# Transposing two bf16 tokens as one 32-bit word, with all inputs loaded as 4 KB pieces, in a gated recurrence kernel

## The chip, the cores and the metric

The kernel runs on one core of one Trainium2 chip. The metric is the device time of one execution in microseconds (us). Engines are called as the profile calls them: PE (matrix multiply; PEld is its weight load), DVE (vector), ACT (activation functions), POOL (GpSimd), SP (it issues the DMAs). Fast executions of one kernel on one chip differ by up to about 1.5% here (316.87 to 321.59 us for the kernel before). Runs further above the fastest of their kernel (up to 327.44) count as slow and are left out of every comparison. A ratio comes with a 95% interval; the record's verdict at a margin of 2% (faster, same, slower, unclear) is given with it.

## The reference

A gated linear recurrence over time, followed by a causal convolution gate and two small matrix products, for 4 sequences of 6336 tokens with 256 channels:

```
a   = exp(8 * sigmoid(r) * log(sigmoid(a_param)))
h_t = a_t * h_(t-1) + sqrt(1 - a_t^2) * sigmoid(i_t) * x_t        (y = h)
out = (sigmoid(conv5(y)) * (y @ w_val)) @ w_out
```

x, r and i (26 MB each) are read and out (26 MB) is written, all in fp32 with a token's 256 channels as one row of 1 KB.

## The kernel before

The inputs arrive with tokens on the 128 partitions. The kernel runs the recurrence with channels on the partitions and time along the row. So PE transposes the tanh of r (for a), the factor n = sqrt(1 - a^2) (back to tokens), and the finished product u (to channels). All engines follow one static order, computed ahead from a table of costs; each engine works its own list strictly in order. Sigmoids are computed as tanh.

```python
nc.sync.dma_start(ri[:, 0, ...], rf[t0:t0 + nt, :].rearrange("(w p j) d -> p w j d", ...))   # r: 4 KB pieces
nc.sync.dma_start(ri[:, 1, ...], if_[t0:t0 + nt, :].rearrange("(k p) d -> p k d", p=P))      # i: 1 KB pieces
nc.sync.dma_start(xt[...],       xf[t0:t0 + nt, :].rearrange("(k p) d -> p k d", p=P))       # x: 1 KB pieces
...
# tanh of r and i in one instruction, 2 x 1024 fp32 elements per partition, to bf16
nc.scalar.activation(out=tring[...], in_=ri[:, :, w, 0:nj, :], func=ACT.Tanh, scale=0.5)
# u2: u = (tanh(i) + 1) * x, per tile on DVE (one instruction) or on POOL (two)
nc.vector.scalar_tensor_tensor(out=u, in0=ti, scalar=1.0, in1=xt, op0=ALU.add, op1=ALU.mult)
nc.gpsimd.tensor_scalar(out=t1, in0=ti, scalar1=1.0, scalar2=1.0, op0=ALU.mult, op1=ALU.add)
nc.gpsimd.tensor_tensor(out=u, in0=t1, in1=xt, op=ALU.mult)
...
for j in range(nj):                                # one bf16 transpose per 128 tokens and half of the channels
    nc.tensor.transpose(out=dst[:, col:col + P], in_=src[:, j, h * P:(h + 1) * P], identity=ident_b[:])
```

i and x come in 1 KB pieces because the scan needs time in order. With token `k*128 + p` on partition `p`, a transposed block is 128 consecutive tokens. With four consecutive tokens per partition, each block would hold every fourth token.

## Time and profile before

| | before |
|---|---|
| time, median (range of 2 runs) | 320.12 us (319.77 to 320.48) |
| span of the profiled run | 317.1 us |
| busy: ACT, DVE, PE, POOL | 290.1, 270.4, 246.2, 224.6 us |
| DMA packets on the main queue | 65904 |

The page and the windows are shown in the prediction. The chain of work that ended last, by engine:

```profile
ACT 25%; DMA 23%; DVE 21%; PE 13%; issue 10%; POOL 4%; SPq 1%; DVEq 0%; ACTq 0%; POOLq 0%
```

Two groups of instructions (line, engine, operation, operands, count | busy us, mean ns | idle before them and what ended it): tanh, and DVE's product with x.

```profile
L351 ACT ACTIVATE tring<-ri 128x2048 bf16<-128x2048 f32 x48 | 90.7, 1919 | 7.7 <-DMA ri<-in_i_gate_dram 7.7
...
L360 DVE SCALAR_TENSOR_TENSOR uring<-tring,xt 128x1024 bf16<-128x1024 bf16 x15 | 24.4, 1624 | 8.2 <-DMA xt<-in_x_dram 8.2
```

And two bursts of PE's transposes from the timeline (start us, length us):

```profile
182.22 1.07 PE L397 MATMUL bank<-ident_b,ering 128*128 128x128 bf16 x16 [0.54 <-ACT ering L388]
...
191.90 1.06 PE L332 MATMUL bank<-ident_b,tring 128*128 128x128 bf16 x16
```

The reader should see that DMA is 23% of the chain of work that ended last. DVE's product lasts 1624 ns on average though its shortest instance takes 1198 ns. Sixteen bf16 transposes take 1.06 us, of which about 0.22 us is the length of the last: (1.06 - 0.22)/15 = 0.056 us each.

### The profile page before, as it was taken

What the parts mean: (1) busy time and instruction counts of PE and PEld (TensorE: products, weight loads), DVE (VectorE), ACT (ScalarE), POOL (GpSimd) and SP (SyncE); (2) the same over time, 40 slices, a digit from 0 to 9 for tenths busy, and PEclk for the clock granted to TensorE, in tenths of its full rate; (3) what the DMA queues carried; (4) which work ended last, traced back from release to release, by engine and by line L of the source; (5) the groups of instructions that cost most, each with busy time, mean ns of one, the idle gap of its engine ahead of it and who ended that gap; (6) DMA issues with size and microseconds to landing.
All of it is one profiled execution on the core that took longest, in us unless ns stands there. A gap on an engine that the chain in (4) does not pass through costs nothing.

```text
span 317.1 us, 7227 instructions
## 1 busy us (share of the span) xinstructions
PE 246.2 (78%) x2987; PEld 163.6 (52%) x2987; DVE 270.4 (85%) x269; ACT 290.1 (91%) x231; POOL 224.6 (71%) x140
## 2 busy tenths in 40 slices
PE   1262877687679768897989798959977997999994
PEld 1141745453546446564655375627644665655662
DVE  3125799999597998999999999997998999999892
ACT  6789999899969999999998999899989999998963
POOL 6329551869469536999989999999997289868000
PEclk9999999999759999999999999997999999999997
DMA  8999999999999999999999999996999994853334
GB/s 208 340 365 380 367 368 382 386 345 352 394 322 349 389 356 375 350 391 385 357 382 382 393 369 383 393 389 191 395 385 383 385 379 164 262 189 133 135 154 179
DMA packets 67327, 104.55 MB, mean 330 GB/s; under 512 B 3287, under 2 KB 54238, under 8 KB 67294
## 3 DMA queue, kind: packets, MB, share of 16 engines
q1 hardware_dynamic: 65904, 103.82, 91.8%
q0 software_dynamic: 1376, 0.26, 1.0%
q8 instruction: 23, 0.38, 0.5%
q14 instruction: 10, 0.08, 0.1%
q10 hardware_dynamic: 14, 0.01, 0.0%
HBM read 78.39 MB, written 25.95 MB: 329 GB/s over the span
## 4 chain that ended last, share of the span: by engine, by line
ACT 25%; DMA 23%; DVE 21%; PE 13%; issue 10%; POOL 4%; SPq 1%; DVEq 0%; ACTq 0%; POOLq 0%
DMA ri<-in_i_gate_dram 15%; DVE yring L425 9%; ACT tring L351 8%; DMA xt<-in_x_dram 6%; DVE gv L477 5%; ACT ering L388 5%; PE bank L489 4%; ACT tg L459 4%; ACT aring L376 4%; PE gp L451 3%; DVE osb L500 3%; PE bank L397 3%; POOL uring L364 2%; DMA ri<-in_r_gate_dram 2%; DVE uring L404 2%
## 5 line engine op out<-in xcount | busy, mean ns | idle before, releaser
L384 POOL TENSOR_TENSOR ering<-aring 128x1024 f32<-128x1024 f32 (+2 forms) x56 | 97.1, 1753 | 55.0 <-ACT aring L376 52.8
L425 DVE TENSOR_TENSOR_SCAN yring<-aring,yring,bank 128x1024 bf16<-128x1024 f32 (+5 forms) x54 | 110.1, 2052 | 0.7 <-PE bank L332 0.5
L351 ACT ACTIVATE tring<-ri 128x2048 bf16<-128x2048 f32 (+1 forms) x51 | 93.9, 1868 | 7.8 <-DMA ri<-in_i_gate_dram 7.7
L364 POOL TENSOR_TENSOR uring<-t,xt 128x1024 bf16<-128x1024 f32 (+1 forms) x36 | 83.6, 2323 | 9.9 <-DMA xt<-in_x_dram 7.3
L451 PE MATMUL gp<-yring,diag 64*64 64x512 bf16 (+14 forms) x1196 | 67.9, 350 | 6.7 <-ACT tg L459 4.6
L489 PE MATMUL bank<-wo,gv 128*128 128x256 bf16 x396 | 57.3, 279 | 18.5 <-DVE gv L477 8.2
L477 DVE SCALAR_TENSOR_TENSOR gv<-tg,val 128x1024 bf16<-128x1024 bf16 (+1 forms) x54 | 60.3, 1120 | 6.7 <-ACT tg L459 4.5
L376 ACT ACTIVATE aring<-bank,khf 128x1024 f32<-128x1024 bf16 (+2 forms) x56 | 59.6, 1111 | 3.3 <-PE bank L332 2.5
L459 ACT ACTIVATE tg<-gp 128x1024 bf16<-128x1024 f32 (+1 forms) x51 | 51.1, 1003 | 7.1 <-PE gp L451 6.8
L489 PEld LDWEIGHTS <-gv 128*128 128x128 bf16 x396 | 36.0, 99 | 37.9 <-issue 16.4
L467 PE MATMUL val<-yring,wv 128*128 128x512 bf16 (+1 forms) x204 | 51.5, 376 | 0.8 <-DVE gv L477 0.8
L500 DVE COPY osb<-bank 128x512 f32<-128x512 f32 x69 | 45.6, 679 | 3.8 <-PE bank L489 3.3
L451 PEld LDWEIGHTS <-diag 64*64 64x64 bf16 x1196 | 30.9, 108 | 33.0 <-issue 16.5
L388 ACT ACTIVATE ering<-ering,b 128x2048 bf16<-128x2048 f32 (+4 forms) x15 | 46.7, 3112 | 0.3
L332 PE MATMUL bank<-ident_b,tring 128*128 128x128 bf16 x396 | 31.3, 231 | 18.5 <-ACT tring L351 13.0
L397 PE MATMUL bank<-ident_b,ering 128*128 128x128 bf16 x396 | 32.9, 240 | 15.8 <-ACT ering L388 12.5
L404 DVE TENSOR_TENSOR uring<-bank,uring 128x1024 bf16<-128x1024 bf16 (+1 forms) x51 | 33.4, 669 | 11.8 <-PE bank L397 11.6
L363 POOL TENSOR_SCALAR t<-tring 128x1024 f32<-128x1024 bf16 (+1 forms) x36 | 40.1, 1115 | 2.6 <-ACT tring L351 1.2
L397 PEld LDWEIGHTS <-ering 128*128 128x128 bf16 x396 | 28.1, 108 | 23.3 <-ACT ering L388 15.5
L332 PEld LDWEIGHTS <-tring 128*128 128x128 bf16 x396 | 25.7, 103 | 27.7 <-ACT tring L351 15.1
L332 PE MATMUL bank<-ident_b,uring 128*128 128x128 bf16 x396 | 30.4, 226 | 3.3 <-DVE yring L425 1.8
L360 DVE SCALAR_TENSOR_TENSOR uring<-tring,xt 128x1024 bf16<-128x1024 bf16 x15 | 24.4, 1624 | 8.2 <-DMA xt<-in_x_dram 8.2
(32 smaller groups left out, 112.6 us busy)
## 6 DMA issues: line engine op xcount, KB each, us to landing
out_dram<-osb SPq DMA_DIRECT2D x48, 512.0 KB, 7.1
ri<-in_r_gate_dram SPq DMA_DIRECT2D x23, 1024.0 KB, 8.1
ri<-in_i_gate_dram SPq DMA_DIRECT2D x23, 1024.0 KB, 11.8
xt<-in_x_dram SPq DMA_DIRECT2D x23, 1024.0 KB, 10.7
ri<-in_r_gate_dram SPq DMA_DIRECT2D x2, 512.0 KB, 5.9
ri<-in_i_gate_dram SPq DMA_DIRECT2D x2, 512.0 KB, 8.1
xt<-in_x_dram SPq DMA_DIRECT2D x2, 512.0 KB, 8.1
ri<-in_r_gate_dram SPq DMA_DIRECT2D x3, 256.0 KB, 2.9
```

Source lines behind the costliest of these rows:

```text
L332: nc.tensor.transpose(out=dst[:, col:col + P], in_=src[:, j, h * P:(h + 1) * P], identity=ident_b[:])
L351: nc.scalar.activation(out=tring[:, r:i + 1:i - r, 0:nj, :], in_=ri[:, :, w, 0:nj, :], func=ACT.Tanh, scale=0.5)
L364: nc.gpsimd.tensor_tensor(out=u, in0=t1, in1=xt, op=ALU.mult)
L376: nc.scalar.activation(out=aring[:, h, a0:a0 + nt].rearrange("c (w p j) -> c w p j", p=P, j=nj), in_=live.pop(("srT", k))[:, 0:nt].rearran ...
L384: nc.gpsimd.tensor_tensor(out=ering[:, h, e0:e0 + nt], in0=a, in1=a, op=ALU.mult)
L388: nc.scalar.activation(out=nring[:, :, 2 * e0:2 * e0 + m], in_=ering[:, :, e0:e0 + m], func=ACT.Sqrt, scale=-0.25, bias=b025[:, 0:1])
L397: nc.tensor.transpose(out=nT[:, j, h * P:(h + 1) * P], in_=nring[:, h, n0 + j * P:n0 + (j + 1) * P], identity=ident_b[:])
L425: nc.vector.tensor_tensor_scan(out=yring[:, h, y0 + c0:y0 + c1], data0=aring[:, h, a0 + c0:a0 + c1], data1=xT[:, c0:c1], initial=0.0 if fr ...
L451: nc.tensor.matmul(out=gp[64 * h:64 * h + 64, m, c0:c1], lhsT=diag[rows, h, kk, rows], rhs=yring[rows, h, src:src + c1 - c0], start=(sh == 0),
L459: nc.scalar.activation(out=tg[:, :, 0:nt], in_=live.pop(("gp", g))[:, :, 0:nt], func=ACT.Tanh, scale=0.5)
L477: nc.vector.scalar_tensor_tensor(out=gv[:, 0:nj, hs, :].rearrange("c j h p -> c j (h p)"), in0=tg[:, hs, 0:nt].rearrange("c h (p j) -> c j ...
L489: nc.tensor.matmul(out=ops[:, e * D:(e + 1) * D], lhsT=gv[:, 2 * i + e, hk, :], rhs=wo[:, hk, :], start=(hk == 0), stop=(hk == H - 1))
```

## The change

A pair of bf16 values of two consecutive tokens is one 32-bit word. PE transposes it as an fp32 element and both tokens stay next to each other. With four tokens per partition that is two word transposes, placed at every second word of the output, and time is in order. So all three inputs can be loaded as 4 KB pieces, and 1188 transposes become 594. The price: tanh and u2 must interleave two tokens, which lie 1 KB apart in the input. a_param is transposed in two 16-bit halves.

```diff
-        nc.sync.dma_start(ri[:, 1, ...], if_[...].rearrange("(k p) d -> p k d", p=P))
+        nc.sync.dma_start(ri[:, 0:nw, 1, 0:nj, :], by_token(if_, c))    # "(w p j) d -> p w j d", r and x alike
 ...
-                for j in range(nj):
-                    nc.tensor.transpose(out=dst[:, col:col + P], in_=src[:, j, h * P:(h + 1) * P], identity=ident_b[:])
+                for w in range(nj // 2):          # src and dst seen as 32-bit words
+                    nc.tensor.transpose(out=dst[:, at + w:at + nw * P:nw],
+                                        in_=src[:, w * D + h * P:w * D + (h + 1) * P], identity=ident_f[:])
 ...                                               # tanh: e, the token of the pair, is innermost
+                out=tring[...].rearrange("p s (w d e) -> p s w d e", d=D, e=2),
+                in_=ri[:, w, :, 0:nj, :].rearrange("p s (w e) d -> p s w d e", e=2), func=ACT.Tanh, scale=0.5)
 ...                                               # u2: xt, ti and u in the same order; on DVE
-                nc.vector.scalar_tensor_tensor(out=u, in0=ti, scalar=1.0, in1=xt, ...)
+                for k in range(nj // 2):
+                    nc.vector.scalar_tensor_tensor(out=u[:, k], in0=ti[:, k], scalar=1.0, in1=xt[:, k], ...)
```

(Not shown: the setup of a_param, nT with words read at every second place, exp reading contiguously. The order of operations and the table of costs are unchanged.)

More of the change, by code (lines that the diff above doesn't have):

```diff
@@ L242, with by_token @@
     live = {}
+    def by_token(src, c):
+        t0, nt, g0, g1 = chunks[c]
+        return src[t0:t0 + nt, :].rearrange("(w p j) d -> p w j d", w=g1 - g0, p=P)
     def load(c):
@@ L247, in load @@
         ri = inp.tile([P, 2, 2, SUB, D], FP32, name="ri", tag="ri", bufs=NIN)
-        nc.sync.dma_start(ri[:, 0, 0:nw, 0:nj, :], rf[t0:t0 + nt, :].rearrange("(w p j) d -> p w j d", w=nw, j=nj))
-        nc.sync.dma_start(ri[:, 1, 0:nw, 0:nj, :].rearrange("p w j d -> p (w j) d"),
-                          if_[t0:t0 + nt, :].rearrange("(k p) d -> p k d", p=P))
+        nc.sync.dma_start(ri[:, 0:nw, 0, 0:nj, :], by_token(rf, c))
+        nc.sync.dma_start(ri[:, 0:nw, 1, 0:nj, :], by_token(if_, c))
         live["ri", c] = ri
@@ L255, in loadx @@
         t0, nt, g0, g1 = chunks[c]
-        xt = inp.tile([P, 2 * SUB, D], FP32, name="xt", tag="xt", bufs=NX)
-        nc.sync.dma_start(xt[:, 0:nt // P, :], xf[t0:t0 + nt, :].rearrange("(k p) d -> p k d", p=P))
+        nw, nj = g1 - g0, nt // (g1 - g0) // P
+        xt = inp.tile([P, 2, SUB, D], FP32, name="xt", tag="xt", bufs=NX)
+        nc.sync.dma_start(xt[:, 0:nw, 0:nj, :], by_token(xf, c))
         live["xt", c] = xt
@@ L271 @@
         make_identity(nc, ident_f[:])
-        ident_b = const.tile([P, P], BF16, name="ident_b")
-        nc.vector.tensor_copy(out=ident_b[:], in_=ident_f[:])
         b025 = const.tile([P, 1], FP32, name="b025")
@@ L288 @@
         with tc.tile_pool(name="ps_setup", bufs=1, space=bass.MemoryType.PSUM) as ps_setup:
-            kps = ps_setup.tile([P, H], FP32, name="kps")
-            nc.tensor.transpose(out=kps[:], in_=ap2[0:H, :], identity=ident_f[0:H, 0:H])
+            U32 = mybir.dt.uint32
+            ap2h = const.tile([H, 2, P], FP32, name="ap2h")
+            nc.vector.tensor_scalar(out=ap2h[:, 0, :].bitcast(U32), in0=ap2[:].bitcast(U32), scalar1=16, scalar2=None,
+                                    op0=ALU.logical_shift_right)
+            nc.vector.tensor_scalar(out=ap2h[:, 1, :].bitcast(U32), in0=ap2[:].bitcast(U32), scalar1=0xFFFF, scalar2=None,
+                                    op0=ALU.bitwise_and)
+            kph = ps_setup.tile([P, 2, H], FP32, name="kph")
+            for k in range(2):
+                nc.tensor.transpose(out=kph[:, k, :], in_=ap2h[0:H, k, :], identity=ident_f[0:H, 0:H])
+            kps = const.tile([P, H], FP32, name="kps")
+            nc.vector.tensor_scalar(out=kps[:].bitcast(U32), in0=kph[:, 0, :].bitcast(U32), scalar1=16, scalar2=None,
+                                    op0=ALU.logical_shift_left)
+            nc.vector.tensor_tensor(out=kps[:].bitcast(U32), in0=kps[:].bitcast(U32), in1=kph[:, 1, :].bitcast(U32),
+                                    op=ALU.bitwise_or)
             kexp = const.tile([P, H], FP32, name="kexp")
@@ L317, with bank @@
         psum = ctx.enter_context(tc.tile_pool(name="psum", bufs=1, space=bass.MemoryType.PSUM))
-        def bank(b, dtype):
-            return psum.tile([P, WIN * 4 // mybir.dt.size(dtype)], dtype, name=f"bank{b}", tag=f"bank{b}", bufs=1)
+        def bank(b):
+            return psum.tile([P, WIN], FP32, name=f"bank{b}", tag=f"bank{b}", bufs=1)
         aring = rings.tile([P, H, NS * WIN], FP32, name="aring")
@@ L323 @@
         nring = ering[:].bitcast(BF16)
-        tring = rings.tile([P, NTR + NTI, SUB, D], BF16, name="tring")
-        uring = rings.tile([P, NU, SUB, D], BF16, name="uring")
+        tring = rings.tile([P, NTR + NTI, SUB * D], BF16, name="tring")
+        tring_w = tring[:].bitcast(FP32)
+        uring = rings.tile([P, NU, SUB * D], BF16, name="uring")
+        uring_w = uring[:].bitcast(FP32)
         yring = rings.tile([P, H, NY * WIN], BF16, name="yring")
         def transposes(dst, srcs, h):
-            col = 0
+            at = 0
             for src, nj in srcs:
-                for j in range(nj):
-                    nc.tensor.transpose(out=dst[:, col:col + P], in_=src[:, j, h * P:(h + 1) * P],
-                                        identity=ident_b[:])
-                    col += P
+                nw = nj // 2
+                for w in range(nw):
+                    nc.tensor.transpose(out=dst[:, at + w:at + nw * P:nw], in_=src[:, w * D + h * P:w * D + (h + 1) * P],
+                                        identity=ident_f[:])
+                at += nw * P
         def op_load(g, eng):
@@ L350, in op_tanh @@
             r, i = g % NTR, NTR + g % NTI
-            nc.scalar.activation(out=tring[:, r:i + 1:i - r, 0:nj, :], in_=ri[:, :, w, 0:nj, :], func=ACT.Tanh, scale=0.5)
+            nc.scalar.activation(
+                out=tring[:, r:i + 1:i - r, 0:nj * D].rearrange("p s (w d e) -> p s w d e", d=D, e=2),
+                in_=ri[:, w, :, 0:nj, :].rearrange("p s (w e) d -> p s w d e", e=2), func=ACT.Tanh, scale=0.5)
         def op_u2(g, eng):
@@ L356, in op_u2 @@
             w = g - chunks[c][2]
-            xt, ti = live["xt", c][:, w * nj:(w + 1) * nj, :], tring[:, NTR + g % NTI, 0:nj, :]
-            u = uring[:, g % NU, 0:nj, :]
+            xt = live["xt", c][:, w, 0:nj, :].rearrange("p (w e) d -> p w d e", e=2)
+            ti = tring[:, NTR + g % NTI, 0:nj * D].rearrange("p (w d e) -> p w d e", d=D, e=2)
+            u = uring[:, g % NU, 0:nj * D].rearrange("p (w d e) -> p w d e", d=D, e=2)
             if eng == "DVE":
-                nc.vector.scalar_tensor_tensor(out=u, in0=ti, scalar=1.0, in1=xt, op0=ALU.add, op1=ALU.mult)
+                for k in range(nj // 2):
+                    nc.vector.scalar_tensor_tensor(out=u[:, k], in0=ti[:, k], scalar=1.0, in1=xt[:, k], op0=ALU.add,
+                                                   op1=ALU.mult)
                 return
-            t1 = work.tile([P, SUB, D], FP32, name="t1", tag="t1", bufs=1)[:, 0:nj, :]
+            t1 = work.tile([P, SUB * D], FP32, name="t1", tag="t1", bufs=1)[:, 0:nj * D].rearrange(
+                "p (w d e) -> p w d e", d=D, e=2)
             nc.gpsimd.tensor_scalar(out=t1, in0=ti, scalar1=1.0, scalar2=1.0, op0=ALU.mult, op1=ALU.add)
@@ L367, in op_srT @@
             c, h = k // 2, k % 2
-            srT = bank(banks["srT", k], BF16)
-            transposes(srT, [(tring[:, g % NTR], tiles[g][1] // P) for g in range(*chunks[c][2:])], h)
+            srT = bank(banks["srT", k])
+            transposes(srT, [(tring_w[:, g % NTR], tiles[g][1] // P) for g in range(*chunks[c][2:])], h)
             live["srT", k] = srT
@@ L374, in op_exp @@
             nt, a0 = chunks[c][1], shape.apos[c]
-            nj = tiles[chunks[c][2]][1] // P
-            nc.scalar.activation(out=aring[:, h, a0:a0 + nt].rearrange("c (w p j) -> c w p j", p=P, j=nj),
-                                 in_=live.pop(("srT", k))[:, 0:nt].rearrange("c (w j p) -> c w p j", p=P, j=nj),
+            nc.scalar.activation(out=aring[:, h, a0:a0 + nt], in_=live.pop(("srT", k))[:].bitcast(BF16)[:, 0:nt],
                                  func=ACT.Exp, scale=khf[:, h:h + 1], bias=khf[:, h:h + 1])
@@ L392, in op_nT @@
             c = chunk_of[g]
-            n0, nt = shape.npos[c] + tiles[g][0] - chunks[c][0], tiles[g][1]
-            nT = bank(banks["nT", g], BF16)[:].rearrange("p (j d) -> p j d", d=D)
+            n0, nw = (shape.npos[c] + tiles[g][0] - chunks[c][0]) // 2, tiles[g][1] // P // 2
+            nT = bank(banks["nT", g])
             for h in range(H):
-                for j in range(nt // P):
-                    nc.tensor.transpose(out=nT[:, j, h * P:(h + 1) * P],
-                                        in_=nring[:, h, n0 + j * P:n0 + (j + 1) * P], identity=ident_b[:])
+                for w in range(nw):
+                    nc.tensor.transpose(out=nT[:, w * D + h * P:w * D + (h + 1) * P],
+                                        in_=ering[:, h, n0 + w:n0 + nw * P:nw], identity=ident_f[:])
             live["nT", g] = nT
         def op_xg(g, eng):
-            nj = tiles[g][1] // P
-            u = uring[:, g % NU, 0:nj, :]
-            nc.vector.tensor_tensor(out=u, in0=live.pop(("nT", g))[:, 0:nj, :], in1=u, op=ALU.mult)
+            n = tiles[g][1] // P * D
+            u = uring[:, g % NU, 0:n]
+            nc.vector.tensor_tensor(out=u, in0=live.pop(("nT", g))[:].bitcast(BF16)[:, 0:n], in1=u, op=ALU.mult)
         def op_xT(k, eng):
             c, h = k // 2, k % 2
-            xT = bank(banks["xT", k], BF16)
-            transposes(xT, [(uring[:, g % NU], tiles[g][1] // P) for g in range(*chunks[c][2:])], h)
+            xT = bank(banks["xT", k])
+            transposes(xT, [(uring_w[:, g % NU], tiles[g][1] // P) for g in range(*chunks[c][2:])], h)
             live["xT", k] = xT
@@ L422, in op_scan @@
             yp = yend(c) - 1
-            xT = live.pop(("xT", k))
+            xT = live.pop(("xT", k))[:].bitcast(BF16)
             for (c0, c1, fresh) in shape.segments(t0, nt):
@@ L485, in op_out @@
             gv = live["gv", g]
-            ops = bank(banks["out", q], FP32)
+            ops = bank(banks["out", q])
             for e in range(2):
```

## The prediction

> **What bounds the kernel now.** I read the first part of the page, which gives busy times, and then the windows of 20 us, because 91% or 85% over a whole span says little about a pipeline with a start and a tail.
>
> ```profile
> PE 246.2 (78%) x2987; PEld 163.6 (52%) x2987; DVE 270.4 (85%) x269; ACT 290.1 (91%) x231; POOL 224.6 (71%) x140
> q1 hardware_dynamic: 65904, 103.82, 91.8%
> ```
>
> ```profile
> core 0: us, PE busy (x) PEld busy (x) DVE busy (x) ACT busy (x) POOL busy (x), PEclk, DMA share, GB/s
> 0.00:20.00 20.00, 6.07 (x47) 3.77 (x47) 5.45 (x23) 14.44 (x16) 10.02 (x18) 1.00 1.02 296
> ...
> 80.00:100.00 20.00, 15.40 (x164) 11.38 (x164) 15.17 (x14) 16.41 (x13) 13.49 (x6) 0.74 1.00 355
> 100.00:120.00 20.00, 13.28 (x156) 8.88 (x153) 18.66 (x20) 19.78 (x14) 9.73 (x6) 1.00 1.03 370
> ...
> 180.00:200.00 20.00, 16.74 (x244) 11.77 (x247) 19.13 (x21) 19.62 (x16) 19.23 (x13) 1.00 1.06 383
> ...
> 220.00:240.00 20.00, 17.63 (x245) 11.64 (x243) 19.27 (x17) 17.57 (x15) 19.49 (x13) 1.00 1.05 376
> ...
> 300.00:320.00 20.00, 11.91 (x157) 7.45 (x156) 10.62 (x15) 8.36 (x14) 0.00 (x0) 0.87 0.33 133
> ```
>
> The reader should see two bounds lying on each other. ACT works nearly all of each middle window, so ACT's 290.1 us plus a start and a tail are a floor. The DMA engines are full (share 1.00 to 1.06) until the last inputs are in. Where ACT has a hole (16.41 of 20 at 80 to 100, 17.57 at 220 to 240) the list of waits names inputs: ACT's tanh waited 7.7 us for the i gate, DVE's product with x 8.2 us and POOL's 7.3 us for x. ACT's idle time is 317.1 - 290.1 = 27 us. By windows 5.6 lies in the first 20 us, 8.7 after 300 us, and about 12.5 between. Two thirds of those 12.5 stand in the windows with input waits: that is what faster loads can win, 8 to 9 us at most.
>
> POOL matters as much: it is 71% busy over all but 19.2 to 19.7 of 20 from 160 to 240 us.
>
> ```profile
> L384 POOL TENSOR_TENSOR ering<-aring 128x1024 f32<-128x1024 f32 x46 | 89.4, 1964 | 46.9 <-ACT aring L376 44.7 <-ACT ering L388 2.2
> L364 POOL TENSOR_TENSOR uring<-t,xt 128x1024 bf16<-128x1024 f32 x33 | 79.8, 2419 | 7.8 <-DMA xt<-in_x_dram 5.3
> ...
> L376 ACT ACTIVATE aring<-bank,khf 128x1024 f32<-128x1024 bf16 x46 | 53.4, 1210 | 2.7 <-PE bank L332 2.5
> L459 ACT ACTIVATE tg<-gp 128x1024 bf16<-128x1024 f32 x48 | 49.4, 1028 | 6.3 <-PE gp L451 6.0
> ```
>
> [...] exp, which today reads PSUM with a step of 256 bytes, pays nothing for the step, and reading contiguously will not make it faster. [...] gv on DVE reads SBUF at a step of 8 bytes[...] and takes 1208 ns for 1024 elements[...]. [...] both POOL products read contiguously now. [...] The trace has fp32 transposes only in the setup[...]:
>
> ```profile
> 3.50 0.37 PE L305 MATMUL wc_ps<-ident_f,wrow 5*128 5x5 f32 x2 [1.11 <-DMA wrow<-in_moe_conv_w_dram]
> ...
> 6.42 0.61 PE L332 MATMUL bank<-ident_b,tring 128*128 128x128 bf16 x4 [2.55 <-ACT tring L351]
> ```
>
> The two fp32 ones last 243 and 265 ns inside a union of 0.37 us, so the second starts about 0.105 us after the first, with a 128-column fp32 weight load between; the four bf16 ones right after start about 0.1 us apart.
>
> **The change part by part.**
>
> *Loads.* i and x go from 1 KB to 4 KB pieces; r and the store have 4 KB already. Half of the 103.8 MB moves in 1 KB pieces. In 300 to 320 us only 4 KB stores move: 133 GB/s at share 0.33, about 400 GB/s at a full share. In the steady window at 100 us it is 370/1.03 = 359. If half the bytes go at 400, the rest goes at 1/(2/359 - 1/400) = 326 (estimate). All at 400 turns 0.918 x 317 = 291 us of DMA time into 291 x 359/400 = 261. That 30 us lies beside the ACT work; on the path it is worth only the 8 to 9 us of holes above. I take 6 to 9.
>
> *PE.* 1188 bf16 transposes become 594 fp32 ones. In steady work 8 bf16 ones take 0.45 to 0.62 us in the chain (56 to 77 ns each), so 1188 x 0.066 = 78 us of array time. At 105 to 210 ns (estimate: the setup spacing, or twice it [...]) it becomes 62 to 125 us. PE is not the bound (17 to 18 of 20), so between -1 and +4 us.
>
> *tanh on ACT.* The same 2048 elements, but the innermost pair of the input now lies 1 KB apart[...]. If free: 0. [...]
>
> *u2 on DVE.* 15 instructions of 1024 become 30 of 512. From gv, (1208 - 418)/(1024 - 256) = 1.03 ns per element and 155 ns fixed, so 15 x 0.155 = 2.3 us more, about half on the path. [...]
>
> *u2 on POOL.* 33 large tiles, input x now in pairs 1 KB apart. [...] About 23 of these tiles start between 120 and 240 us, where POOL is full[...]: +12 to +17 on the path.
>
> *Start.* a_param goes through four more small DVE instructions (0.17 us each, 0.2 apart as in the setup now) and one more transpose: about 0.9 us before the first table load, which directly precedes the first tanh at 5.31. The second tanh waits 1.96 us for its input at 9.89, so half is hidden: +0.4.
>
> Sum with free reads: -7.5 + 1 (PE) + 1.2 (DVE) + 0.4 = -5 us, about 315; with PE on its cheap side, about 312. Sum with only POOL paying: -5 + 15, about 330, less what the retained slack gives back. I put the median at 317.
>
> **Rivals.** *ACT pays for the stepped read:* about 320 + 84 - 8 = 396. [...] Against: exp reads PSUM at 256 bytes, and gv reads PSUM at 16 bytes, without a penalty[...]. I give it 18%. *POOL becomes the bound from 140 to 240 us:* 322 to 338. For it: [...] POOL is already at 96 to 98% there. [...] 40%. *Nothing pays and the loads help:* 308 to 316, 42%. *The faster loads are worth nothing* because DVE (over 19 of 20 in five windows) takes over: 317 to 320, part of the last case. [...]
>
> **Range and chances.** Faster by 2% means below 313.7: 0.42 x 0.65 and a little from the rest, 0.30. Slower means above 326.5: 0.18 from ACT plus about half of POOL's 0.40, 0.38. The rest is 0.32. The distribution has a far lobe near 395 which I leave out; the range is 307 to 348.
>
> **What would show it right or wrong.** The tanh row: 1919 ns again, or about 3600. The POOL product with x: 2419 ns or 3.2 us and more, with POOL at 20 of 20 from 140 to 240. The DVE product: 30 rows near 680 ns. DMA: packets down from 65904 to about 27000, and the GB/s row near 390 to 400 while it is full, or the share under 1 if the engines no longer ask for more. The first tanh at about 6.2 us. fp32 transposes spaced 100 to 210 ns. The waits for i and x mostly gone. The prediction is wrong if the gain exceeds 13 us, since ACT's own 290 us stay; then some ACT instruction got shorter, which I exclude.

## The result, and the profile after

The changed kernel takes 334.88 us (334.85 to 334.91, 2 runs) against 320.12: ratio 1.046, interval 1.041 to 1.051. Here and below a ratio is the mean time of one kernel's fast runs over that of the other's of the same rounds, so it is not quite the ratio of the medians.

From the page after: engines, main DMA queue, and the chain that ended last.

```profile
PE 256.4 (77%) x2394; PEld 162.0 (49%) x2394; DVE 282.3 (85%) x287; ACT 312.4 (94%) x231; POOL 231.8 (70%) x140
...
q1 hardware_dynamic: 28272, 103.82, 83.0%
...
ACT 42%; DVE 19%; PE 17%; issue 14%; DMA 5%; POOL 2%; DVEq 0%; ACTq 0%; SPq 0%
```

The loads did what they should: packets fell from 65904 to 28272, and DMA fell from 23% of the chain to 5%. Yet ACT's busy time rose by 22.3 us and DVE's by 11.9. The span rose by 15.9 us, which is ACT's 22.3 us less 6.4 us of idle time that ACT lost; this is bookkeeping and names no cause. The groups say which instructions grew:

```profile
L372 ACT ACTIVATE tring<-ri 128x2048 bf16<-128x2048 f32 x48 | 113.2, 2391 | 0.0
...
L391 POOL TENSOR_TENSOR uring<-t,xt 128x1024 bf16<-128x1024 f32 x33 | 89.3, 2706 | 5.0 <-DMA xt<-in_x_dram 2.3
...
L385 DVE SCALAR_TENSOR_TENSOR uring<-tring,xt 128x512 bf16<-128x512 bf16 x30 | 35.5, 1222 | 4.3 <-DMA xt<-in_x_dram 4.3
```

Tanh went from 1919 to 2391 ns and no longer waits for inputs (0.0 for 7.7). POOL's product went from 2419 to 2706 ns. DVE's product, a half tile now, takes 1222 ns, where a free half takes 673. The timeline of DVE (before, then twice after), and that of POOL after, show when the half tiles are long:

```profile
44.85 1.78 DVE L360 SCALAR_TENSOR_TENSOR uring<-tring,xt 128x1024 bf16<-128x1024 bf16 x1
...
43.05 1.29 DVE L385 SCALAR_TENSOR_TENSOR uring<-tring,xt 128x512 bf16<-128x512 bf16 x2
...
45.38 4.28 DVE L385 SCALAR_TENSOR_TENSOR uring<-tring,xt 128x512 bf16<-128x512 bf16 x2
```

```profile
44.90 4.21 POOL L409 TENSOR_TENSOR ering<-aring 128x1024 f32<-128x1024 f32 x2 [6.16 <-ACT aring L402]
```

The first pair of halves, with POOL idle, takes 1.29 us. The second pair lasts until 49.66 us, half a microsecond after POOL's two instructions end at 49.11. (What stands in brackets is POOL's idle time before, and what ended it.) Its counterpart in the kernel before, one whole tile, started at 44.85 while POOL was at the same work (43.33 to 48.39 us), and was done in 1.78 us. It is so over the whole run: the six pairs of halves that started with POOL idle took 1.29 to 1.31 us, the nine beside POOL's work 1.52 to 4.28 us; of the whole tiles before, those beside POOL took at most 2.48 us (the shortest of all 1.20). The trace does not name what a half waits for; that it is POOL's work is read from these times. e11 below tests the split, not the cause.

PE's bursts after:

```profile
178.20 1.04 PE L353 MATMUL bank<-ident_f,tring 128*128 128x128 f32 x8
...
194.30 1.22 PE L422 MATMUL bank<-ident_f,ering 128*128 128x128 f32 x8 [0.48 <-ACT ering L413]
```

Eight word transposes take as long as sixteen bf16 ones: (1.04 - 0.30)/7 = 0.106 us each with the group's mean of 305 ns for the last, and (1.22 - 0.32)/7 = 0.13 for n, whose words are read at every second place. (The first of the two bursts writes every second word in PSUM, and is the shorter.) Three windows of 20 us (columns as in the prediction):

```profile
80.00:100.00 20.00, 14.02 (x86) 9.44 (x87) 18.14 (x16) 16.67 (x10) 11.43 (x7) 0.74 0.81 315
...
180.00:200.00 20.00, 16.73 (x173) 10.39 (x173) 18.34 (x21) 19.94 (x14) 18.33 (x11) 1.00 0.94 359
...
220.00:240.00 20.00, 15.94 (x162) 10.09 (x161) 19.87 (x17) 19.63 (x14) 18.88 (x11) 0.91 0.87 309
```

In these windows DMA is no longer full (share 0.81 to 0.94): the loads of r and i waited 51.6 us in all for tanh to free their buffer, against 35.0 before. At 220 to 240 us ACT's hole of 2.4 us is gone (19.63); the one at 80 to 100 stays.

### The profile page after: what moved, and what is told of

Its sections match the earlier page's. It is cut to its first block, busy times and chain, and to the rows that moved or that the text cites. A ratio compares the mean times of both kernels' runs of the same rounds, so it can differ in the third digit from the quotient of the medians.

```text
span 333.0 us, 6087 instructions
## 1 busy us (share of the span) xinstructions
PE 256.4 (77%) x2394; PEld 162.0 (49%) x2394; DVE 282.3 (85%) x287; ACT 312.4 (94%) x231; POOL 231.8 (70%) x140
## 3 DMA queue, kind: packets, MB, share of 16 engines
q1 hardware_dynamic: 28272, 103.82, 83.0%
## 4 chain that ended last, share of the span: by engine, by line
ACT 42%; DVE 19%; PE 17%; issue 14%; DMA 5%; POOL 2%; DVEq 0%; ACTq 0%; SPq 0%
ACT tring L372 17%; DVE yring L450 9%; ACT aring L402 7%; ACT ering L413 6%; ACT tg L484 6%; PE gp L476 5%; DVE gv L502 4%; PE bank L514 4%; PE bank L422 3%; PE bank L353 3%; DMA xt<-in_x_dram 3%; ACT L413 3%; DVE osb L525 2%; DVE uring L385 2%; DMA ri<-in_r_gate_dram 2%
## 5 line engine op out<-in xcount | busy, mean ns | idle before, releaser
L372 ACT ACTIVATE tring<-ri 128x2048 bf16<-128x2048 f32 (+1 forms) x51 | 117.0, 2326 | 0.0
L391 POOL TENSOR_TENSOR uring<-t,xt 128x1024 bf16<-128x1024 f32 (+1 forms) x36 | 93.5, 2598 | 5.2 <-DMA xt<-in_x_dram 2.3
L476 PE MATMUL gp<-yring,diag 64*64 64x512 bf16 (+14 forms) x1196 | 69.9, 360 | 5.1 <-ACT tg L484 3.3
L353 PE MATMUL bank<-ident_f,tring 128*128 128x128 f32 x198 | 34.7, 305 | 20.4 <-ACT tring L372 15.0
L422 PE MATMUL bank<-ident_f,ering 128*128 128x128 f32 x198 | 34.6, 316 | 15.4 <-ACT ering L413 10.1
L390 POOL TENSOR_SCALAR t<-tring 128x1024 f32<-128x1024 bf16 (+1 forms) x36 | 37.9, 1054 | 3.6 <-ACT tring L372 2.4
L422 PEld LDWEIGHTS bank<-ident_f,ering 128*128 128x128 f32 x198 | 28.6, 209 | 23.8 <-ACT ering L413 12.3
L353 PEld LDWEIGHTS bank<-ident_f,tring 128*128 128x128 f32 x198 | 23.4, 151 | 33.5 <-ACT tring L372 19.9
L385 DVE SCALAR_TENSOR_TENSOR uring<-tring,xt 128x512 bf16<-128x512 bf16 x30 | 35.5, 1222 | 4.3 <-DMA xt<-in_x_dram 4.3
L353 PE MATMUL bank<-ident_f,uring 128*128 128x128 f32 x198 | 31.0, 286 | 4.9 <-DVE uring L429 2.9
```

What stands on the lines that cost most here:

```text
L353: nc.tensor.transpose(out=dst[:, at + w:at + nw * P:nw], in_=src[:, w * D + h * P:w * D + (h + 1) * P], identity=ident_f[:])
L372: nc.scalar.activation(out=tring[:, r:i + 1:i - r, 0:nj * D].rearrange("p s (w d e) -> p s w d e", d=D, e=2), in_=ri[:, w, :, 0:nj, :].rea ...
L422: nc.tensor.transpose(out=nT[:, w * D + h * P:w * D + (h + 1) * P], in_=ering[:, h, n0 + w:n0 + nw * P:nw], identity=ident_f[:])
L476: nc.tensor.matmul(out=gp[64 * h:64 * h + 64, m, c0:c1], lhsT=diag[rows, h, kk, rows], rhs=yring[rows, h, src:src + c1 - c0], start=(sh == 0),
```

## The experiments

The theory after reading the trace was simple: tanh's 23 us of extra ACT work on the bound are the loss. Rivals: the products with x, or the transposes. The first four runs shared one chip and the runs of the kernel before on it (322.1 us median); e5 to e8 ran on a second chip (321.6), e9 to e12 on that same chip in later rounds (320.3). "Wrong" kernels keep the work and the waits and take elements in another order; where a kernel also undoes DVE's split (e2, e5, e7, e9, e10) or the longer setup (e9, e10), the instruction count falls with it.

### e1: tanh as its elements lie

```diff
-                in_=ri[:, w, :, 0:nj, :].rearrange("p s (w e) d -> p s w d e", e=2), ...
+                in_=ri[:, w, :, 0:nj, :].rearrange("p s j d -> p s (j d)"), ...   # and the output so
```

> Only the tanh of the changed kernel is altered: it reads its 2048 elements in the order in which they lie and writes them so (the pairs are then the wrong ones, so the result is wrong on purpose); both products with x keep their stepped reads. Theory (the stepped fp32 read costs ACT 0.23 ns per element, 48 x 0.47 + 0.7 = 23 us of ACT work on the bound): tanh back to 1919 ns, ACT busy near 290 us, time 312 to 318 us. Rival (POOL's and DVE's longer products carry the loss): tanh back to 1919 ns but time still above 326 us. Rival (the fp32 transposes on PE carry it): time above 326 us as well, ACT waiting for PE.

337.0 us, ratio 1.045 (1.040 to 1.050): wrong, and no faster than the change. From the page and the groups:

```profile
PE 253.9 (76%) x2366; PEld 164.4 (49%) x2394; DVE 283.3 (85%) x287; ACT 291.2 (87%) x231; POOL 232.7 (70%) x140
```

```profile
L372 ACT ACTIVATE tring<-ri 128x2048 bf16<-128x2048 f32 x48 | 90.4, 1914 | 15.0 <-POOL t L390 4.7 <-POOL ering L409 4.1 <-DVE uring L385 3.5
```

Tanh is back to 1914 ns and ACT to 291.2 us busy, but ACT now idles: tanh waits 15.0 us, mostly for POOL and DVE. The first step of POOL's product (t) and DVE's product free the ring that tanh writes; the 4.1 us put down to POOL's squaring of a (ering) name an instruction that stands in the same list of POOL. The theory fell: without tanh's cost, something else is enough for the whole loss.

### e2: the products as their elements lie too

The products lose their stepped views, and DVE has one instruction per tile again (`out=u, in0=ti, in1=xt` over 1024 elements).

> As the run before, and the products with x on DVE and POOL read and write in the order in which elements lie too, one instruction on DVE again (wrong result on purpose). What stays of the change is the fp32 transposes, the 4 KB loads and the longer setup. Theory: 307 to 313 us, DVE busy back near 271 us, POOL product 2.37 us. If the products' lengthening costs nothing because ACT is the bound: within 1% of the run before. If fp32 transposes cost PE and its readers more than the loads give: above 318 us.

322.3 us, ratio 1.002 (0.998 to 1.006), wrong; the theory's 307 to 313 us was missed. ACT is busy 290.9 us, DVE 268.1, POOL 225.1. So the whole loss lies in the interleaving and the split that came with it, and 4 KB loads with word transposes give nothing together.

### e3 and e4: interleave on the output

Two correct kernels: every input is walked row by row, and the bf16 output is written at every second place; in e3 for tanh only, in e4 also for the products.

```diff
+                out=tring[...].rearrange("p s (w d e) -> p e s w d", d=D, e=2),
+                in_=ri[:, w, :, 0:nj, :].rearrange("p s (w e) d -> p e s w d", e=2), ...
```

> A correct kernel: tanh walks the input row by row (reads step 4 bytes) and interleaves on its output instead (bf16 writes 4 bytes apart). Theory (it is the read that jumps 1 KB between two streams that costs): tanh near 1.92 us and a time like that of the first run, 312 to 318 us. Rival (interleaving costs ACT on whichever side it is done): tanh 2.3 us or more and 330 us or more.

> A correct kernel: tanh as in the run before, and the products with x also read x row by row and write bf16 pairs 4 bytes apart; DVE does two instructions of 512 per tile, one per token of the pair. Theory: POOL product back to 2.37 us (from 2.65), DVE still near 282 us busy because the split, not the step, lengthens it [...]; time 308 to 315 us. Rival (POOL pays for stepped bf16 writes instead): product over 2.6 us.

339.3 us (1.054, interval 1.050 to 1.058) and 338.6 us (1.053, 1.048 to 1.058): both slower than the kernel before, and no better than the change; both theories (312 to 318 and 308 to 315 us) were missed. Tanh took 2526 and 2533 ns: ACT pays more for bf16 writes 4 bytes apart than for the stepped read (2391). POOL's product came back to 2415 ns, so POOL pays for the read and not for such a write. But with ACT busy 317.7 us that gained nothing.

### e5, e6, e7: one stepped operation at a time

From e2, one operation at a time got its stepped form back: tanh (e5), DVE's product with its split (e6), POOL's product (e7). All are wrong.

> The changed kernel with only its tanh stepped; both products with x go through the elements as they lie, DVE in one instruction per tile (wrong result on purpose). The run without any stepped operand took 322 us and the run with only the products stepped 337. If the tanh's 23 us of ACT work alone are enough for the loss too (two causes beside each other, each sufficient): 330 to 336 us, ACT busy 312 us. If the products are the whole loss and ACT has room: 322 to 325 us.

> Tanh and POOL's product as they lie; only DVE's product with x is stepped and split into two instructions of 512 (wrong result on purpose). If DVE's 15 split tiles carry the products' loss (DVE busy 283 in place of 268[...]): 330 us or more. If POOL's 0.28 us per tile carries it: 320 to 325 us.

> Tanh and DVE's product as they lie, DVE in one instruction; only POOL's product with x is stepped (wrong result on purpose). If POOL carries the products' loss: 330 us or more; by its sum of 24 tiles x 0.28 = 7 us in the stretch where POOL is full: 327 to 331. If DVE carries it: 321 to 325 us.

| stepped | time, us | ratio to before (interval) |
|---|---|---|
| none (e2) | 322.3 | 1.002 (0.998 to 1.006) |
| POOL (e7) | 327.8 | 1.029 (1.018 to 1.039) |
| DVE, split (e6) | 331.3 | 1.038 (1.028 to 1.049) |
| DVE and POOL (e1) | 337.0 | 1.045 (1.040 to 1.050) |
| tanh (e5) | 337.2 | 1.057 (1.048 to 1.067) |
| all (the change) | 334.9 | 1.046 (1.041 to 1.051) |

Each alone costs 2.6 to 5.5 points over e2, and all three no more than the largest, so the costs do not add. That they lie beside each other, each engine's longer work filling waits on another, is argued from the waits (15.0 us of tanh in e1, 11.3 in e6, 7.3 in e7), not isolated. The rows come from two chips: e5, e6 and e7 are "unclear" by the record's verdict, and against e10 below, which is e2 with the old setup on their own chip (1.007, 0.998 to 1.015), POOL's step alone stands out least. e6 and e7 met their expectations; tanh alone (ACT busy 312.6 us) came out 1 us above the 330 to 336 that e5 expected. The DVE group of e6 and the POOL group of e7:

```profile
L389 DVE SCALAR_TENSOR_TENSOR uring<-tring,xt 128x512 bf16<-128x512 bf16 x30 | 39.4, 1353 | 5.3 <-DMA xt<-in_x_dram 3.3 <-ACT tring L372 2.0
```

```profile
L391 POOL TENSOR_TENSOR uring<-t,xt 128x1024 bf16<-128x1024 f32 x33 | 88.7, 2687 | 3.5 <-DMA xt<-in_x_dram 0.8
```

### e8: the 4 KB loads alone

In the kernel before, i and x get r's source order and nothing else changes (wrong).

> The kernel before with nothing changed but the source order of the loads of i and x, which become 4 KB pieces like r (tokens out of order, wrong result on purpose). Prediction on record: 6 to 9 us faster, 311 to 315 us. What the run without stepped operands suggests: nothing, 318 to 322 us, with the DMA share falling under 1 because buffers come free no earlier, POOL full from 140 to 240 us as before.

315.5 us, ratio 0.989 (0.979 to 0.999), unclear: a gain of about 1%, 3 to 4 us, half of what I predicted, though the interval reaches from next to nothing to 6.7 us. In these windows DMA is still full, at a higher rate, and so is POOL:

```profile
160.00:180.00 20.00, 16.92 (x196) 10.39 (x198) 19.33 (x20) 19.60 (x14) 19.58 (x12) 1.00 1.02 401
...
220.00:240.00 20.00, 16.36 (x206) 10.91 (x206) 18.34 (x19) 17.89 (x15) 19.29 (x11) 1.00 1.02 412
```

From 220 to 240 us the GB/s rose from 376 to 412, and ACT's hole stayed (17.89 where it was 17.57). It is still a wait for i, as these lines of ACT's timeline (before, then e8) show:

```profile
232.60 3.71 ACT L351 ACTIVATE tring<-ri 128x2048 bf16<-128x2048 f32 x2 [1.56 <-DMA ri<-in_i_gate_dram]
...
230.28 3.71 ACT L353 ACTIVATE tring<-ri 128x2048 bf16<-128x2048 f32 x2 [1.73 <-DMA ri<-in_i_gate_dram]
```

So the higher rate did not bring this load in before tanh wanted it. Over the whole run tanh's wait for i fell from 7.7 to 4.2 us, about what the kernel gained. ACT's other hole, at 80 to 100 us, stands beside waits for PE in both kernels (2.0 and 1.5 us before, 1.9 and 2.0 in e8); behind them DVE had waited for x, 3.40 us before and 2.91 in e8.

### e9 and e10: the transposes alone, and with the loads

e9 is the kernel before with word transposes and contiguous elements (1 KB loads). e10 adds the 4 KB loads. Both have the old setup of a_param and are wrong.

> The kernel before with only its transposes changed: 594 of fp32 words in place of 1188 of bf16, with the 1 KB loads, the old setup and no stepped read by ACT, DVE or POOL (wrong result on purpose). My prediction gave PE -1 to +4 us. If the transposes eat what the 4 KB loads give (the run with both stood at 322, the one with the loads alone at 315.5): 324 to 329 us. If they are neutral: 318 to 322.

> As the run before with the 4 KB loads as well and the old setup: the changed kernel without stepped operands and without the longer setup (wrong result on purpose). If the setup's 0.4 us is all that the setup costs: 319 to 322 us. If the transposes are neutral after all and it was the chip that differed: 314 to 317.

324.5 us, ratio 1.013 (1.008 to 1.018), and 321.8 us, ratio 1.007 (0.998 to 1.015). So the word transposes cost about 4 us, which eats the loads' gain. Two waits of the kernel before, and of e9, show where (engine and line, what it waited for: us in all, times, longest):

```profile
DVE uring L404 <- PE bank L397: 11.6, 15, 4.1
ACT tg L459 <- PE gp L451: 6.8, 8, 2.0
...
DVE uring L415 <- PE bank L408: 15.8, 17, 4.2
ACT tg L470 <- PE gp L462: 12.4, 14, 2.9
```

PE's burst is as long as before, but a group's first word arrives later: the mean length of a transpose went from 226-240 ns to 288-314. That this added latency is what ACT and DVE wait for is argued from these waits; no run isolates it.

### e11: the split alone

```diff
-                nc.vector.scalar_tensor_tensor(out=u, in0=ti, scalar=1.0, in1=xt, ...)
+                for k in range(nj // 2):
+                    s = slice(2 * k, 2 * k + 2)
+                    nc.vector.scalar_tensor_tensor(out=u[:, s], in0=ti[:, s], scalar=1.0, in1=xt[:, s], ...)
```

> The kernel before (correct) with DVE's product with x done as two instructions of 512 per tile, nothing stepped. If the split itself [...]: mean of a half above 0.9 us where 0.68 is its free time, DVE busy up by 5 to 12 us, time 323 us or more. If it is the step [...]: mean 0.7 to 0.85 us, DVE busy up by 2 to 4 us, time within 1% of before.

A correct kernel, 330.2 us, ratio 1.028 (1.021 to 1.036). Nothing is stepped in it, and yet:

```profile
L362 DVE SCALAR_TENSOR_TENSOR uring<-tring,xt 128x512 bf16<-128x512 bf16 x30 | 39.8, 1370 | 6.3 <-DMA xt<-in_x_dram 6.3
```

Halves of 1370 ns where 665 is the shortest, and DVE busy 285.4 us for 270.4. The split, not the step, lengthens DVE's product. The step is free for DVE: the shortest stepped half took 673 ns in the changed kernel.

### e12: what ACT pays for which step

Four read patterns of tanh by tile number, one run of unknown state (wrong on purpose; its time, 357.9 us, says nothing, but the change's own pattern takes 2377 ns here for 2391, so the lengths can be compared).

> The changed kernel with four read patterns of tanh by tile number (wrong result on purpose): single elements from two streams 1 KB apart as in the change; runs of two elements from two streams; a step of 16 bytes; a step of 8 bytes. [...] If what costs is a read that isn't the neighbour of the one before: 2.39, about 2.15, 2.39 and 2.39 us.

The groups, in order: a step of 16 bytes; single elements from two streams 1 KB apart; a step of 8 bytes; runs of two elements from two streams 4 KB apart.

```profile
L378 ACT ACTIVATE tring<-ri 128x2048 bf16<-128x2048 f32 x12 | 47.3, 3944 | 2.4 <-POOL ering L419 2.1 <-POOL t L400 0.3
L382 ACT ACTIVATE tring<-ri 128x2048 bf16<-128x2048 f32 x12 | 28.5, 2377 | 0.3
L380 ACT ACTIVATE tring<-ri 128x2048 bf16<-128x2048 f32 x12 | 25.0, 2081 | 0.0
L376 ACT ACTIVATE tring<-ri 128x2048 bf16<-128x2048 f32 x12 | 24.3, 2028 | 3.3 <-DMA ri<-in_i_gate_dram 2.1 <-DVE uring L395 1.0
```

Against 1919 ns contiguous, runs of two elements (2028 ns) and a step of 8 bytes (2081) cost 6 to 8%, and a step of 16 bytes (3944) doubles the time. The change's pattern, single elements from two streams (2377), lies between, at 24%. The times expected for a read that isn't the neighbour of the one before fit only the change's own pattern (2.39 us) and, more loosely, the runs of two (2.15): the step of 16 bytes took far longer than 2.39 us, the step of 8 bytes less. What sets these lengths was not shown.

No run points to a correct kernel that beats the kernel before. Only e8 did, with its tokens out of order, and no run puts them in order without interleaving. One rival stays untested: the order of operations, the table of costs and the choice of DVE or POOL for each product were all kept from the kernel before. No run recomputes them with the longer tanh and products, so how much of the loss a new order would win back is open.

## Why the prediction was right or wrong

The time lies in the range of 307 to 348 and "slower" had the largest chance, 0.38, but the median of 317 was 18 us too low. That the range held is in good part luck: the 0.38 was made of a tanh twice as long and of a POOL with no time to spare from 140 to 240 us. Tanh grew by a quarter, POOL had 0.4 to 1.7 us to spare in each 20 us there (18.33 to 19.57 busy), and two of the three costs that the runs show, a part-way penalty of tanh and DVE's split, were in no sum. Step by step:

- **What bounds the kernel.** Half right. ACT's work was a floor. Of the 8 to 9 us of holes that faster loads were to fill, tanh's wait for i gave back 3.5 us in e8 (7.7 to 4.2). The hole at 80 to 100 us stood beside waits for PE, not beside an input wait of ACT, and the one at 220 to 240 remained with DMA at 412 GB/s. (The DMA share was not 1.00 to 1.06 throughout: three windows before 220 us that are not shown have 1.08, 1.07 and 0.90.)
- **Loads.** Right in kind (28272 packets, DMA share under 1), mis-sized on the path: "I take 6 to 9" measured about 1%, 3 to 4 us, in e8, where the interval does not exclude 6.
- **PE.** The low estimate of the spacing was right (0.106 us, 0.13 for n; 396 x 0.106 + 198 x 0.13 = 68 us, against 1188 x 0.056 = 67 in such bursts before, so nothing saved). That was luck: the two setup transposes it was read from move 5 columns each (5x5 in their line), not 128, so they say nothing of a block of 128. The doubling that I allowed for in the upper estimate did not come: the burst that writes every second word in PSUM is the one with 0.106 us. The path term "-1 to +4" measured about +4 in e9.
- **tanh on ACT.** The first step that failed. I gave it two outcomes, free or at half its rate, and put 18% on the second. Half the rate is an estimate: tanh's rows before take 1919 ns for 2048 elements and 1056 ns for 1024, so 0.84 ns each, and 48 x 2048 and 3 x 1024 of them make about 85 us, near the 84 in the rival's sum. The two instructions held against that rival show no such cost in the traces: exp takes 1210 ns where it reads PSUM at a step of 256 bytes and 1216 ns after the change, where it reads it contiguously; gv, at 8 bytes in SBUF and 16 in PSUM, takes 1208 ns where DVE's product of the same size, as its elements lie, takes 1198 at the shortest. But neither is a read of SBUF by ACT, and tanh did pay: 23 us of ACT work (90.7 to 113.2 for the large tiles), between the two, and alone it makes 337 us (e5).
- **u2 on DVE.** The step that failed next. "15 x 0.155 = 2.3 us more" counted only the fixed cost of an instruction. It measured 11.1 us (24.4 to 35.5), because a pair of halves beside POOL's work takes up to 4.28 us, where a whole tile took at most 2.48. e11 shows the cost of the split alone: 2.8%.
- **u2 on POOL.** Right in kind, mis-sized: 2706 ns per tile, 0.29 us more than 2419, where I named 3.2 us and more. That figure, and the 12 to 17 us on the path, were estimates of mine; no trace before the change had such a read. It still cost more on the path than I gave for its size: 2.6 points in e7.
- **Start.** First tanh at 5.71 us, so +0.4 where I predicted +0.9 before any hiding.
- **Rivals.** The sum "with only POOL paying", 330, comes near the result but for a wrong reason: its 15 us for POOL were that estimate, which no run shows, and three engines pay, each alone enough for more than half of it (2.6, 3.6 and 5.5 of 4.6 points). The sum with free reads and the cheap PE gives 313, not 312, which changes nothing.

## What to carry to other kernels

In this kernel, where several engines are nearly full in one static order, lengthening any of three moved the end, and their costs did not add: undoing one of them showed nothing, so undo all, then put them back one at a time. Before trading layout for larger transfers, ask which engine will interleave, and measure that engine's rate for exactly that step. Before splitting an instruction, look in the timeline for an engine beside whose work it takes longer: here the split alone cost 2.8%.
